# Pairing 64-row matmuls in the first product of a float32r feed-forward

## The chip, the cores and the metric

The kernel runs on one core of one Trainium2 chip. The metric is device time in microseconds (us) of one execution; a smaller number is better. TensorE does the matmuls, VectorE (DVE), ScalarE (ACT) and GpSimd (POOL) the elementwise work, and SyncE (SP) issues most of the DMAs.

## The reference

```python
def _moe2_ref(x, w_in, w_out):                    # the part that is changed
    h = np.maximum(x @ w_in, 0.0)                 # x: 3072 x 320, w_in: 320 x 2048
    return (h * h @ w_out).astype(np.float32)     # w_out: 2048 x 320

def reference(**kwargs):
    attn_out = _attn_ref(**attn_kwargs)           # a recurrence over 768 steps, 4 x 8 heads of 40
    x = attn_out, as 3072 tokens x 320
    x = _moe_ref(x=x, **moe_kwargs)               # first feed-forward: (x@w1 * x@w2) @ w3 @ w_out
    return _moe2_ref(x=x, **moe2_kwargs)          # second feed-forward
```

All inputs are float32.

## The kernel before, in words

The program has three parts that overlap at their seams: the recurrence in chunks of 32 steps, the first feed-forward, whose matmuls are laid between the chunks, and the second feed-forward at the end. The change is in the second one and in the preparation of its weights.

**Numbers in two parts.** Matmuls of the feed-forwards run in float32r. For accuracy each operand is split into a high and a low part, and a product is three matmuls: high by high, high by low, low by high.

**The first product.** The 320 rows of contraction are 128 + 128 + 64. Each of the two blocks of 128 rows takes three matmuls (tiles `wih`, `wil` for the weights, `xh`, `xl` for the data). The last 64 rows share one tile: `wir` holds on its 128 partitions the high part of 64 rows of weights and the low part of the same 64 rows. For the first 1024 hidden units the high part lies on partitions 0 to 63, for the other 1024 on partitions 64 to 127; the low part lies on the other half. `xq[:, 0]` holds the high part of the data's last 64 rows on both halves, and `xq[:, 1]` the low part on both halves. So `wir` by `xq[:, 0]` gives high by high plus low by high, and `wir` by `xq[:, 1]` gives high by low plus low by low. That makes eight matmuls (the helper `dense`, line 370) into one PSUM bank `ph` of 128 hidden units by 512 tokens.

**The loop.** It runs over `j` (6 groups of 512 tokens) and `ff` (16 blocks of 128 hidden units). `b_h(j, ff)` makes one `ph`; ScalarE takes the Relu out of it (`r_`, line 981), VectorE squares it (`q_`), ScalarE casts the square to the high part `rh`, VectorE subtracts for the low part `rl`. `b_o(j, ff)` adds the block's share to four accumulators `po` of 128 tokens by 320, three matmuls of 320 columns for each (line 997). `b_o` follows `b_h` by LAG = 3 blocks. There are four banks for `ph` and four for `po`. After the last block of a group of tokens the four `po` banks are copied out to `ob` (line 1007), two copies on VectorE and two on ScalarE, before the next group of tokens may write them.

**Who sets the order.** In the first parts TensorE's order is written by hand. In the second feed-forward the framework's planner sets it at build time: by a model of times it takes, for each engine, the earliest instruction in program order whose inputs and banks it holds to be ready. An engine then runs its instructions in that fixed order and waits where one is not ready.

**Weight preparation.** Before the loop, eight chunks of 256 hidden units are fetched and split (`split_w` for `wih` and `wil`, `wu` for the second product's `wuh` and `wul`). A chunk takes GpSimd, ScalarE and VectorE instructions on its way. `split_r` prepares 256 columns of each half of `wir` at a time, in the first four of the eight chunks. This work shares its engines with the end of the first feed-forward, whose matmuls are released between the chunks by `fill.pull`.

**Matmuls on a part of the array.** The recurrence has matmuls with a `tile_position`, which use only a part of the rows or columns of the array: line 772 (104 rows by 64 columns, two column tiles in turn), line 597 (40 rows by 32 columns, eight tiles: two halves of the rows, `tile_position=(64 * y, 32 * b)`, with y changing fastest, by four groups of columns). They are in float32, where one `matmul` call appears as two MATMUL rows in the trace.

Of the kernel before, what the change touches and what calls it, by code (L numbers as in the profile page):

```python
# [7 lines left out]
F32 = mybir.dt.float32  # L8
# [14 lines left out]
NU = B * H  # L23
HZ = H // 2
LAG = 3
LEAST, MOST = 0.25, 2.0

OPENING = (
# [35 lines left out]
LOOK = (1, 0, 2, 1, 5, 2)  # L64
# [179 lines left out]
def body(tc, img, rv, rd, vn, vp, raw, w1, w2, w3t, wo, win, wo2, ident, maskt, out, dbg=None):  # L244
    nc = tc.nc
    mm = nc.tensor.matmul
    act, dve, pool, sp = nc.scalar, nc.vector, nc.gpsimd, nc.sync

    with (
# [12 lines left out]
        with right, tc.manual_schedule(engines={mybir.EngineType.PE}):  # L262
# [99 lines left out]
            def dense(ps, w_, ff, xh, xl, xq, i0=0, i1=8):  # L362
                h, l, r = w_
                f = slice(128 * ff, 128 * ff + 128)
                seq = []
                for k in range(2):
                    seq += [(h[:, k, f], xh[:, k]), (h[:, k, f], xl[:, k]), (l[:, k, f], xh[:, k])]
                seq[5:5] = [(r[:, f], xq[:, 0]), (r[:, f], xq[:, 1])]
                for i in range(i0, i1):
                    mm(out=ps, lhsT=seq[i][0], rhs=seq[i][1], start=(i == 0), stop=(i == 7))  # L370
# [544 lines left out]
            wih = wb.tile([128, 2, FB], F32R, name="wih")  # L915
            wil = wb.tile([128, 2, FB], F32R, name="wil")
            wir = wb.tile([128, FB], F32R, name="wir")
            wuh = wb.tile([128, 16, DM], F32R, name="wuh")
            wul = wb.tile([128, 16, DM], F32R, name="wul")
            xt = {}  # L920
# [25 lines left out]
            wst = tc.alloc_tile_pool(name="wst", bufs=1, side="left")  # L946
            early = False
            bufs.update(raw=BB[0], wst=BB[1])
            for j in range(8):
                for k in range(2):  # L950
                    split_w(wst, win, wih, wil, j, k)
                if j < 4:
                    split_r(wst, [(win, 256 * j + 1024 * i, wir) for i in range(2)])
                for k in (2 * j, 2 * j + 1):
                    wu(wst, k)
                if j == 0:
                    b_split(wb, 0, 1)
                fill.pull(BP)
            fill.pull()
# [2 lines left out]
        with (  # L962
            left,
            tc.tile_pool(name="mb", bufs=1, side="right") as mb,
            tc.tile_pool(name="ps_h", bufs=4, space=PSUM) as ps_h,
            tc.tile_pool(name="ps_o", bufs=1, space=PSUM) as ps_o,
        ):
            NB = NTOK // 512
            tc.mark_branch_hint_location("wide", hint="LikelyTaken",
                                         engines=[mybir.EngineType.SP, mybir.EngineType.Activation,  # L970
                                                  mybir.EngineType.DVE])
            rr, last = {}, []

            def b_h(j, ff):
                ps = ps_h.tile([128, 512], F32, name="ph")
                dense(ps, (wih, wil, wir), ff, *xt[j])
                r_ = mb.tile([128, 512], F32, name="r_", bufs=2)
                q_ = mb.tile([128, 512], F32, name="q_", bufs=2)
                rh = mb.tile([128, 512], F32R, name="rh", bufs=4)
                rl = mb.tile([128, 512], F32R, name="rl", bufs=4)  # L980
                act.activation(out=r_, in_=ps, func=AF.Relu)
                dve.tensor_tensor(out=q_, in0=r_, in1=r_, op=ALU.mult)
                last[:] = [act.copy(out=rh, in_=q_).ins,
                           dve.tensor_tensor(out=rl, in0=q_, in1=rh, op=ALU.subtract).ins]  # L984
                rr[ff] = (rh, rl)

            po = {}

            def b_o(j, ff, gs=range(4)):
                if ff == 0:  # L990
                    po[j] = [ps_o.tile([128, DM], F32, name=f"po{g}") for g in range(4)]
                rh, rl = rr[ff]
                for g in gs:
                    t = slice(128 * g, 128 * g + 128)
                    for i, (a_, b_) in enumerate(((rh[:, t], wuh[:, ff]), (rh[:, t], wul[:, ff]),
                                                  (rl[:, t], wuh[:, ff]))):
                        mm(out=po[j][g], lhsT=a_, rhs=b_, start=(ff == 0 and i == 0), stop=(ff == 15 and i == 2))  # L997
                if ff == 15:
                    for g in gs:
                        c = 4 * j + g  # L1000
                        if j < NB - 1:
                            ob = mb.tile([128, DM], F32, name="ob", bufs=4)
                        else:
                            if g == 0:
                                po["ob"] = mb.tile([128, 4, DM], F32, name="oball", bufs=1)
                            ob = po["ob"][:, g]
                        (act.copy if g % 2 else dve.tensor_copy)(out=ob, in_=po[j][g])
                        if j < NB - 1:
                            sp.dma_start(out=out.rearrange("(b s) o -> b s o", b=B)[:, C * c:C * c + C], in_=ob)
                    if j == NB - 1 and gs[-1] == 3:  # L1010
                        for b in range(B):
                            (act if b % 2 else sp).dma_start(
                                out=out.rearrange("(b c s) o -> b s c o", b=B, s=C)[b][:, 4 * j:4 * j + 4],
                                in_=po["ob"][C * b:C * b + C])

            NW = 8
            nw = NU * S * D // 128 // NW
            low, high = (mb.tile([128, NW], F32, name=n, bufs=1) for n in ("low", "high"))

            def look(i):  # L1020

                w_ = mb.tile([128, nw], F32, name="w_", bufs=2)
                sp.dma_start(out=w_, in_=raw[3].rearrange("u s d -> (u s d)").rearrange("(p f) -> p f", p=128)[
                    :, nw * i:nw * i + nw])
                for o, op in ((low, ALU.min), (high, ALU.max)):
                    with tc.issue_after(last[1]):
                        dve.tensor_reduce(out=o[:, i:i + 1], in_=w_, axis=mybir.AxisListType.X, op=op)
                    yield

            def within():  # L1030


                with tc.issue_after(last[1]):
                    for o, op in ((low, ALU.min), (high, ALU.max)):
                        dve.tensor_reduce(out=o[:, 0:1], in_=o, axis=mybir.AxisListType.X, op=op)
                    dve.tensor_scalar(out=high[:, 0:1], in0=high[:, 0:1], scalar1=MOST, scalar2=None, op0=ALU.is_le)
                    dve.scalar_tensor_tensor(out=low[:, 0:1], in0=low[:, 0:1], scalar=LEAST, in1=high[:, 0:1],
                                             op0=ALU.is_ge, op1=ALU.mult)
                row = mb.tile([1, 128], F32, name="row", bufs=1)
                sp.dma_start(out=ok_d, in_=low[:, 0:1])  # L1040
                sp.dma_start(out=row, in_=ok_d.rearrange("p o -> o p"))
                for _ in range(4):
                    yield
                one = mb.tile([1, 1], mybir.dt.int32, name="one", bufs=1)
                with tc.issue_after(last[1]):
                    dve.tensor_reduce(out=row[:, 0:1], in_=row, axis=mybir.AxisListType.X, op=ALU.min)
                    dve.tensor_copy(out=one, in_=row[:, 0:1])
                yield one

            def guard():  # L1050

                for i in range(NW):
                    yield from look(i)
                yield from within()

            lag, steps, fast = [], guard(), None
            for j in range(NB):
                for ff in range(16):
                    if (j, ff) == LOOK[4:6]:
                        fast = nc.values_load(fast, min_val=0, max_val=1)  # L1060
                    if ff == 4 and j + 1 < NB:
                        b_load(mb, j + 1)
                    if ff == 12 and j + 1 < NB:
                        with tc.issue_after(last[0]), tc.issue_after(last[1]):
                            b_split(mb, j + 1)
                    b_h(j, ff)
                    if LOOK[0:2] <= (j, ff) and ff % LOOK[2] == LOOK[3]:
                        fast = next(steps, fast)
                    lag.append((j, ff))
                    if len(lag) > LAG:  # L1070
                        b_o(*lag.pop(0))
            for g in range(4):
                with tc.high_priority(offset=FIRST * (4 - g)):
                    for it in lag:
                        b_o(*it, gs=(g,))
# [61 lines left out]
```

## Time and profile before

| what | value |
|---|---|
| median of 3 runs | 1070.16 us (1068.26 to 1074.72) |
| the profiled execution's own time | 1071.28 us |
| its span, first to last instruction | 1069.5 us |
| TensorE busy | 918.1 us, 86% of the span |
| VectorE, ScalarE, GpSimd busy | 712.5, 443.8, 233.2 us |
| mean granted TensorE clock | 0.961 |

Times in the rows are microseconds from the start of the span, unless marked ns. PE is TensorE's matmul stream, PEld its weight loads. Matmuls are pipelined and their ends are modelled, so a row's own duration is longer than the pitch at which matmuls follow one another; the pitch is read from the starts.

### The profile page before, as it was taken

How to read it: one execution, taken by the hardware profiler on the slowest of the kernel's cores; microseconds unless marked ns; L12 is line 12 of the kernel's file. 1: busy time of each engine (PE TensorE's matmuls, PEld its weight loads, DVE VectorE, ACT ScalarE, POOL GpSimd, SP SyncE). 2: the span in 40 equal slices, each digit the busy share in tenths (PEclk: the TensorE clock that was granted, in tenths of full speed). 3: DMA queues.
4: the chain of work that ended last, by engine and by line, in shares of the span. 5: the costliest groups of instructions: out<-in, count | busy, mean ns of one | idle time of the engine just before them, and what ended most of it. 6: DMA issues, size and time to landing. Idle time of an engine off the chain costs nothing.

```text
span 1069.5 us, 29225 instructions
## 1 busy us (share of the span) xinstructions
PE 918.1 (86%) x12240; PEld 822.5 (77%) x12240; DVE 712.5 (67%) x1399; ACT 443.8 (41%) x942; POOL 233.2 (22%) x304
## 2 busy tenths in 40 slices
PE   1327777688989889979899999889999999999997
PEld 1315545588888878979798889868989898898896
DVE  6864879957975997798489444887456554444432
ACT  2424556343434423424343434775334333333332
POOL 0271224433343343533200000652000000000000
PEclk9999888899999999989899999989999999999999
DMA  8976785666666567766644542665122121000001
GB/s 212 307 235 177 209 247 158 171 168 170 163 154 173 148 151 182 170 170 149 164 118 110 136 96 60 171 188 111 30 62 53 59 48 25 2 25 1 18 8 28
DMA packets 208922, 134.45 MB, mean 126 GB/s; under 512 B 143741, under 2 KB 184062, under 8 KB 208368
## 3 DMA queue, kind: packets, MB, share of 16 engines
q1 hardware_dynamic: 201424, 110.61, 40.6%
q0 software_dynamic: 7072, 21.57, 7.1%
q8 instruction: 99, 1.62, 0.7%
q10 hardware_dynamic: 288, 0.33, 0.2%
q14 instruction: 39, 0.32, 0.1%
HBM read 99.27 MB, written 33.19 MB: 124 GB/s over the span
## 4 chain that ended last, share of the span: by engine, by line
PE 48%; DVE 26%; DMA 12%; issue 5%; ACT 4%; POOL 3%; SPq 2%; ACTq 0%; DVEq 0%; POOLq 0%
PE ph L370 16%; PE po L997 15%; PE ab L370 6%; DMA im<-img 5%; DVE tmp L656 4%; PE px L428 4%; DVE T L659 4%; PE pat L800 2%; DVE RX L808 2%; DVE yst L812 2%; DVE gl L408 2%; DVE g L402 1%; DVE wst L328 1%; DVE YI L777 1%; POOL im L584 1%
## 5 line engine op out<-in xcount | busy, mean ns | idle before, releaser
L997 PE MATMUL po<-wul,rh 128*128 128x320 f32 x384 | 118.3, 308 | 0.0
L997 PE MATMUL po<-wuh,rh 128*128 128x320 f32 x384 | 118.0, 308 | 0.0
L997 PE MATMUL po<-wuh,rl 128*128 128x320 f32 x384 | 116.9, 308 | 0.0
L407 ACT CAST gh<-g 128x256 fp32r<-128x256 f32 x96 | 39.0, 406 | 99.8 <-DVE g L402 86.5
L370 PE MATMUL ph<-xh,wih 128*128 128x512 f32 x192 | 76.0, 396 | 0.7 <-issue 0.7
L428 PE MATMUL px<-wph,gh 128*128 128x320 f32 x192 | 68.1, 355 | 9.3 <-DVE x L433 4.8
L370 PE MATMUL ph<-xh,wil 128*128 128x512 f32 x192 | 75.7, 394 | 0.0
L370 PE MATMUL ph<-xl,wih 128*128 128x512 f32 x192 | 75.6, 394 | 0.0
L997 PEld LDWEIGHTS po<-wul,rh 128*128 128x128 f32 x384 | 72.0, 188 | 4.2
L997 PEld LDWEIGHTS po<-wuh,rh 128*128 128x128 f32 x384 | 72.0, 188 | 3.8
L997 PEld LDWEIGHTS po<-wuh,rl 128*128 128x128 f32 x384 | 71.6, 188 | 0.6 <-DVE rl L984 0.6
L800 PE MATMUL pat<-YI,YR 128*40 128x72 f32 (+1 forms) x1536 | 58.8, 240 | 13.7 <-DVE qt L602 8.1
L800 PEld LDWEIGHTS pat<-YI,YR 128*40 128x40 f32 x1536 | 54.5, 127 | 19.2 <-DVE qt L602 9.7
L408 DVE TENSOR_TENSOR gl<-g,gh 128x256 fp32r<-128x256 f32 x96 | 48.2, 503 | 30.0 <-ACT gh L407 29.6
L401 ACT COPY a_sb<-ab 128x256 f32<-128x256 f32 x96 | 35.6, 371 | 76.4 <-PE ab L370 75.9
L656 DVE TENSOR_TENSOR tmp<-PT,T 128x31 f32<-128x31 f32 (+20 forms) x170 | 64.9, 382 | 3.4
L659 DVE TENSOR_TENSOR T<-T,tmp 128x31 f32<-128x31 f32 (+20 forms) x170 | 64.5, 380 | 3.0
L428 PE MATMUL px<-wph,gl 128*128 128x320 f32 x192 | 63.2, 329 | 3.4 <-DVE gl L408 3.4
L584 POOL TENSOR_TENSOR im<-im,suf 104x256 f32<-104x256 f32 x80 | 64.4, 836 | 0.0
L428 PE MATMUL px<-wpl,gh 128*128 128x320 f32 x192 | 62.4, 325 | 0.0
L370 PE MATMUL ph<-xq,wir 128*128 128x512 f32 x192 | 60.1, 394 | 0.0
L370 PE MATMUL ab<-xh,w1h 128*128 128x256 f32 x192 | 57.9, 302 | 2.5 <-ACT xh L357 2.2
(539 smaller groups left out, 2444.3 us busy)
## 6 DMA issues: line engine op xcount, KB each, us to landing
raw<-w3t SPq DMA_DIRECT2D x16, 512.0 KB
YR<-KB_d SPq DMA_DIRECT2D x48, 160.0 KB
im<-img POOLq DMA_DIRECT2D x28, 240.0 KB, 4.5
wt<-AW_d SPq DMA_DIRECT2D x24, 214.5 KB
raw<-wo SPq DMA_DIRECT2D x16, 320.0 KB
RX<-vp SPq DMA_DIRECT2D x24, 208.0 KB
vs<-rv SPq DMA_DIRECT2D x24, 208.0 KB
KB_d<-kn POOLq DMA_DIRECT2D x14, 320.0 KB, 5.3
```

Of the source, the lines that this page charges most:

```text
L370: mm(out=ps, lhsT=seq[i][0], rhs=seq[i][1], start=(i == 0), stop=(i == 7))
L401: act.copy(out=a_sb, in_=ps[:, 0])
L407: act.copy(out=t["gh"][:, ff], in_=g)
L408: dve.tensor_tensor(out=t["gl"][:, ff], in0=g, in1=t["gh"][:, ff], op=ALU.subtract)
L428: mm(out=ps, lhsT=a_, rhs=b_, start=(k == 0 and i == 0), stop=(k == 7 and i == 2))
L584: eng.tensor_tensor(out=kb[:, g, :, :, j], in0=kb[:, g, :, :, j], in1=sg, op=ALU.mult)
L656: dve.tensor_tensor(out=tv, in0=Pv[:, :, s, s + 1:n].unsqueeze(3).to_broadcast(sh), in1=Tv[:, :, s, 0:s + 1].unsqueeze(2).to_broadcast(sh) ...
L659: return dve.tensor_tensor(out=o, in0=o, in1=tv, op=ALU.subtract).ins
L800: mm(out=ps[64 * y:64 * y + D, b, 72 * z:72 * z + n], lhsT=YR[:, u], rhs=YI[:, u, 0:n], start=True, stop=True, tile_position=(0, 64 * y))
L808: dve.tensor_tensor(out=o, in0=v[r, :, :, C:72], in1=decay.unsqueeze(3).to_broadcast([D, 2, HZ, D]), op=ALU.mult)
L812: dve.tensor_tensor(out=yst[r, :, 2 * g:2 * g + 2].rearrange("p z b t -> p b z t"), in0=v[r, :, :, 0:C], in1=wt[c][r, 2 * g:2 * g + 2, :, ...
L997: mm(out=po[j][g], lhsT=a_, rhs=b_, start=(ff == 0 and i == 0), stop=(ff == 15 and i == 2))
```

## The change: pairs of 64-row matmuls, four blocks at a time

The eighth matmul, `wir` by `xq[:, 1]` over 128 rows, is replaced by a matmul over the 64 rows that hold the high part of the weights alone (the low by low share is left out of the sum). `tile_position` places it on the upper or the lower half of the array's rows. Blocks are visited in a new order (`ORDER`: 0, 8, 1, 9, 2, 10, ...), so that neighbours have their high parts on different halves. At every fourth block `b_r` takes all four `ph` banks and issues the four 64-row matmuls of the next four blocks, upper, lower, upper, lower, as the ones that start the accumulation. The other seven matmuls of each block follow in `b_h` as before. The chunks of weights are prepared in the order 0, 4, 1, 5, 2, 6, 3, 7, with `split_r` at every second one.

```diff
+ORDER = tuple(f + 8 * h for i in range(0, 8, 2) for f in (i, i + 1) for h in range(2))
...
-            for j in range(8):
+            for m in range(8):
+                j = m // 2 + 4 * (m % 2)
                 for k in range(2):
                     split_w(wst, win, wih, wil, j, k)
-                if j < 4:
+                if m % 2 == 0:
                     split_r(wst, [(win, 256 * j + 1024 * i, wir) for i in range(2)])
                 for k in (2 * j, 2 * j + 1):
                     wu(wst, k)
...
-            def b_h(j, ff):
-                ps = ps_h.tile([128, 512], F32, name="ph")
-                dense(ps, (wih, wil, wir), ff, *xt[j])
+            def b_r(j, n):
+                for m in range(n, n + 4):
+                    ph[m] = ps_h.tile([128, 512], F32, name="ph")
+                for m in range(n, n + 4):
+                    r = slice(64 * (m % 2), 64 * (m % 2) + 64)
+                    mm(out=ph[m], lhsT=wir[r, 128 * ORDER[m]:128 * ORDER[m] + 128], rhs=xt[j][2][r, 1],
+                       start=True, stop=False, tile_position=(64 * (m % 2), 0))
+
+            def b_h(j, n):
+                if n % 4 == 0:
+                    b_r(j, n)
+                ps, ff = ph.pop(n), ORDER[n]
+                f = slice(128 * ff, 128 * ff + 128)
+                xh, xl, xq = xt[j]
+                seq = [(wir[:, f], xq[:, 0])]
+                for k in range(2):
+                    seq += [(wih[:, k, f], xh[:, k]), (wih[:, k, f], xl[:, k]), (wil[:, k, f], xh[:, k])]
+                for i, (a_, b_) in enumerate(seq):
+                    mm(out=ps, lhsT=a_, rhs=b_, start=False, stop=(i == 6))
...
-                rr[ff] = (rh, rl)
+                rr[n] = (rh, rl)
...
-                for ff in range(16):
+                for n in range(16):
...
-                    b_h(j, ff)
+                    b_h(j, n)
```

`b_o` takes its weights at `ORDER[n]` and starts and stops the accumulation at n = 0 and n = 15.

## Rows read from the trace of the kernel before

**Rows 1.** The page: the span, and each engine's busy time

```profile
span 1069.5 us, 29225 instructions
PE 918.1 (86%) x12240; PEld 822.5 (77%) x12240; DVE 712.5 (67%) x1399; ACT 443.8 (41%) x942; POOL 233.2 (22%) x304
```

**Rows 2.** Busy time by stretch: length, each engine, granted clock, DMA share, GB/s

```profile
700.00:716.00 16.00, 11.13 (x45) 9.22 (x45) 13.24 (x26) 11.37 (x32) 9.24 (x10) 0.79 0.56 175
716.00:732.00 16.00, 15.95 (x82) 13.70 (x81) 15.65 (x24) 13.21 (x32) 6.91 (x8) 1.00 0.98 214
732.00:1062.00 330.00, 330.00 (x1830) 297.34 (x1830) 159.09 (x230) 123.06 (x205) 2.04 (x2) 1.00 0.13 30
```

**Rows 3.** The chain that ended last, 912 to 916: start, duration, what

```profile
912.05 1.87 PE ph L370 x8
913.92 1.76 PE po L997 x12
```

**Rows 4.** Groups by shape: line 772, busy, mean ns

```profile
L772 PE MATMUL pat<-RT,vs 104*64 104x64 f32 x768 | 29.3, 233 | 6.1 <-ACT vs L761 5.9
```

**Rows 5.** TensorE's timeline around one run of line 772: start, duration

```profile
387.25 0.28 PE L370 MATMUL ab<-xh,w1l 128*128 128x256 f32 x1
387.37 0.28 PE L370 MATMUL ab<-xh,w1h 128*128 128x256 f32 x1
387.57 1.15 PE L772 MATMUL pat<-RT,vs 104*64 104x64 f32 x32
388.65 0.39 PE L370 MATMUL ab<-xl,w1h 128*128 128x256 f32 x1
388.88 0.41 PE L370 MATMUL ab<-xq,w1r 128*128 128x256 f32 x2
```

**Rows 6.** TensorE's timeline around one run of line 597

```profile
393.50 0.85 PE L597 MATMUL pat<-im 40*32 40x64 f32 x64 [0.58 <-DVE YI L777]
394.27 0.39 PE L370 MATMUL ab<-xl,w2h 128*128 128x256 f32 x1
394.50 0.41 PE L370 MATMUL ab<-xq,w2r 128*128 128x256 f32 x2
```

**Rows 7.** Timeline of a regular block, ScalarE and TensorE

```profile
913.52 0.40 PE L370 MATMUL ph<-xh,wil 128*128 128x512 f32 x1
914.02 0.60 ACT L981 ACTIVATE r__12360<-ph 128x512 f32<-128x512 f32 x1 [1.65 <-PE ph L370]
915.52 0.40 PE L370 MATMUL ph<-xh,wih 128*128 128x512 f32 x1
```

**Rows 8.** Timeline where the accumulators change from tokens 0 to 1

```profile
777.64 0.40 PE L370 MATMUL ph<-xh,wih 128*128 128x512 f32 x1
...
778.17 0.42 ACT L1007 COPY ob<-po 128x320 f32<-128x320 f32 x1
...
779.28 0.39 PE L370 MATMUL ph<-xh,wil 128*128 128x512 f32 x1
779.51 0.39 PE L370 MATMUL ph<-xh,wih 128*128 128x512 f32 x1
...
781.15 0.31 PE L997 MATMUL po<-wuh,rh 128*128 128x320 f32 x1
```

**Rows 9.** Timeline of the loop's start, TensorE

```profile
714.08 0.47 PE L370 MATMUL ph<-xh,wih 128*128 128x512 f32 x1 [0.66 <-issue]
...
714.61 0.39 PE L370 MATMUL ph<-xh,wil 128*128 128x512 f32 x1
714.84 0.39 PE L370 MATMUL ph<-xh,wih 128*128 128x512 f32 x1
...
724.81 0.31 PE L997 MATMUL po<-wuh,rh 128*128 128x320 f32 x1
```

**Rows 10.** Timeline of the loop's start, ScalarE

```profile
720.25 0.61 ACT L983 CAST rh<-q__10605 128x512 fp32r<-128x512 f32 x1
...
724.14 0.61 ACT L981 ACTIVATE r__10655<-ph 128x512 f32<-128x512 f32 x1
```

More of the change, by code (lines that the diff above doesn't have):

```diff
@@ L955, in body @@
                     wu(wst, k)
-                if j == 0:
+                if m == 0:
                     b_split(wb, 0, 1)
@@ L984, in b_h, with b_o @@
                            dve.tensor_tensor(out=rl, in0=q_, in1=rh, op=ALU.subtract).ins]
-                rr[ff] = (rh, rl)
-            po = {}
-            def b_o(j, ff, gs=range(4)):
-                if ff == 0:
+                rr[n] = (rh, rl)
+            po, ph = {}, {}
+            def b_o(j, n, gs=range(4)):
+                ff = ORDER[n]
+                if n == 0:
                     po[j] = [ps_o.tile([128, DM], F32, name=f"po{g}") for g in range(4)]
-                rh, rl = rr[ff]
+                rh, rl = rr[n]
                 for g in gs:
@@ L996, in b_o @@
                                                   (rl[:, t], wuh[:, ff]))):
-                        mm(out=po[j][g], lhsT=a_, rhs=b_, start=(ff == 0 and i == 0), stop=(ff == 15 and i == 2))
-                if ff == 15:
+                        mm(out=po[j][g], lhsT=a_, rhs=b_, start=(n == 0 and i == 0), stop=(n == 15 and i == 2))
+                if n == 15:
                     for g in gs:
@@ L1057, in body @@
             for j in range(NB):
-                for ff in range(16):
-                    if (j, ff) == LOOK[4:6]:
+                for n in range(16):
+                    if (j, n) == LOOK[4:6]:
                         fast = nc.values_load(fast, min_val=0, max_val=1)
-                    if ff == 4 and j + 1 < NB:
+                    if n == 4 and j + 1 < NB:
                         b_load(mb, j + 1)
-                    if ff == 12 and j + 1 < NB:
+                    if n == 12 and j + 1 < NB:
                         with tc.issue_after(last[0]), tc.issue_after(last[1]):
                             b_split(mb, j + 1)
-                    b_h(j, ff)
-                    if LOOK[0:2] <= (j, ff) and ff % LOOK[2] == LOOK[3]:
+                    b_h(j, n)
+                    if LOOK[0:2] <= (j, n) and n % LOOK[2] == LOOK[3]:
                         fast = next(steps, fast)
-                    lag.append((j, ff))
+                    lag.append((j, n))
                     if len(lag) > LAG:
```

## The prediction

> **What bounds the kernel now.** I read the page first: TensorE is busy for 86% of the span, more than any other engine [rows 1]. An average over stages decides nothing, so the table by stretch came next. From 732 to 1062 us TensorE is busy for all of 330 us at a granted clock of 1.00, while VectorE and ScalarE work for 159 and 123 us [rows 2]. The chain of waits agrees: there it runs from TensorE to TensorE, eight matmuls into `ph` in 1.87 us, then twelve into `po` in 1.76 us, with nothing between [rows 3]. So in the loop of the second feed-forward each nanosecond of TensorE's is one of the kernel's, and there alone the change works. The loop's first 16 us are nearly as full, 15.95 of 16 [rows 2], but there ScalarE and VectorE are full too (13.21 and 15.65), with weight preparation. Before it, from 700 to 716, TensorE idles for 4.9 us.
>
> **The change, part by part.**
>
> *The unit price.* A full 512-column matmul costs 1.87 / 8 = 0.234 us of TensorE. There are 6 x 16 = 96 blocks, so 24 groups of four. A group gives up four full matmuls, 4 x 0.234 = 0.934 us, and gets four 64-row ones.
>
> *Do two halves run at the same time?* No row of before shows float32r on a half. Line 597 uses two halves of the rows by four groups of columns, in float32. First what one such matmul costs its tile: line 772's 32 rows take 1.15 us [rows 5], the last of them 0.23 [rows 4], so the pitch is (1.15 - 0.23) / 31 = 0.030; two column tiles take turns, so a 64-column one holds its tile for 0.059. Line 597 has the same 64 columns, and passes 64 of them in the 0.77 us from its first start to the next line's [rows 6]: 64 x 0.059 / 0.77 = 4.9 at once. Four groups of columns alone give four, so the halves overlapped. I take that over for float32r: two pairs cost 2 x 0.234 = 0.467. The bounds are 4 x 0.234 = 0.934 (one after the other) and 2 x 0.227 = 0.454 (the pitch at the loop's start: 45 matmuls from 714.61 to the first `po` at 724.81 [rows 9]).
>
> *What going into the part-array mode and out of it costs.* Around line 772, from the last full matmul's start (387.37) to the second full one's after it (388.88) is 1.51 us [rows 5]. Two full matmuls at 0.12 (387.25 to 387.37) and 16 turns of 0.059 explain 0.24 + 0.95 = 1.19, so 0.32 us is lost at the two seams. A part of it can be seen: the first full matmul after the block is followed after 0.23 instead of 0.12, and after line 597 it is 0.23 again [rows 6], so about 0.11 us is the load of 128 columns of weights that no longer hides behind the matmul ahead. Line 772 loads 64 columns on its way in, the change loads 128 on both ways, so I take between 0.32 and 0.43, and settle on 0.40.
>
> The Trainium skill has a rule that speaks against this change: "TensorEngine Tiling (Array Packing)", Tiling Modes, Key Properties, says that a change of tiling mode, not merely of tile, drains the engine. The trace agrees with it by the 0.32 us above. Another page of the Trainium skill, "TensorE: Matmul & The Clock Gate", Part 3, gives a pack of tiles as one matmul's duration plus some 4 ns for each further tile, with no charge for the seams. By that formula alone a group would cost an estimated 0.47 us; the trace does not bear it out.
>
> *A regular group* then costs 0.40 + 0.467 = 0.867 against 0.934: 0.067 us gained. Half of the four matmuls' time is saved, 0.467, and 0.40 is paid back for one trip into the half-array mode.
>
> *The four banks.* `b_r` claims all four `ph` banks together, so its fourth matmul waits for the Relu of the block just finished; before, a block waited for a Relu three blocks old. In a regular place the cover is enough: a block's last matmul starts at 913.52, its Relu runs from 914.02 to 914.62, and the next block's first matmul comes at 915.52, after twelve matmuls into `po` [rows 7]. That leaves 0.9 us. Behind the waiting matmul stands all of TensorE's queue, so if the cover goes, it costs that wait directly.
>
> *The cover is gone where the accumulators change.* There the planner held `b_o` of the new tokens' block 0 for not ready (its banks are still being copied out, the fourth copy at 778.17), and put matmuls of two blocks in a row: from 777.64 over 779.28, where block 3's last one starts, and on with block 4 from 779.51, with `po` only at 781.15 [rows 8]. After the change the next work in program order behind block 3 is `b_r` of blocks 4 to 7. Three of its matmuls have free banks. The fourth waits for block 3's Relu, which starts some 0.1 us after that block's end and takes 0.60 [rows 7], while the three take about 0.47. So the planner fills in full matmuls of block 4, and the fourth goes alone: two trips, 0.867 + (0.40 + 0.234) = 1.50 us against 0.934. That is 0.57 lost, at the five changes of tokens: 2.8 us. The bounds: 0.067 gained each, if the planner waits and the Relu is early; 0.57 lost.
>
> *The loop's start.* Block 0's group finds free banks. For the second group TensorE arrives at 714.08 + 0.87 + 28 x 0.227 = 721.3, and block 3's Relu ended at 724.75 in the trace, because ScalarE was full [rows 10]. Before, TensorE filled this time with blocks 4 and 5 and first came to `po` at 724.81 [rows 9]. Now it has the high parts of block 0's `po` (its `rh` is ready at 720.86 [rows 10], 8 x 0.147 = 1.2 us) and blocks 4 and 5, if `b_r` is taken apart. I charge one extra trip as above, 0.57; bounds 0.07 gained, and 3.4 lost (nothing fills it).
>
> *The order of the weight chunks.* Block n needs chunk number n / 2 as before, only under other names, so supply does not get later; two of four `split_r` move from ahead of the loop to its first 16 us. What that shifts in the end of the first feed-forward is the planner's affair. Its bound is the idle time there, 4.9 us of 16 [rows 2], gained or lost in part; I take 0 and keep 2 us to either side. The DMA count is unchanged.
>
> *The sum*, against the profiled execution's own 1071.28 us: 18 regular groups, 18 x 0.067 = -1.2; five token changes, +2.8; the start, +0.6; chunks 0. Together +2.2, 1073.5. The median of the runs is 1.1 us under the profiled one, so on its scale 1072.4; I say **1073**.
>
> **The rivals.**
>
> *The seams stay whole.* The planner keeps each `b_r` together everywhere. Then 24 x 0.067 = 1.6 us are gained, 1069.7; with 0.32 for a trip and 0.227 for a pair, 24 x (0.934 - 0.774) = 3.8, 1067.4. For it: all regular blocks follow program order. Against: the token changes in the trace are out of it [rows 8].
>
> *The halves do not overlap in float32r*, and the change doesn't do what it says. Then a group costs 0.40 + 0.934 and the kernel becomes **slower**: 24 x 0.40 = 9.6, 1080.9, and with six more trips of 0.40, 1083.3. It decides from a pair's time: above (0.934 - 0.40) / 2 = 0.267 us, in place of 0.234, even a regular group loses. For it: no row with float32r on half an array. Against: line 597 [rows 6].
>
> *The seams cost nothing*: the weights of the first pair, and of the first full matmul after it, load behind the matmul ahead, and the two pairs' 0.467 us are the whole price of a group. 24 x 0.467 = 11.2 us gained, 1060.1. Against it stand the 0.32 us around line 772 and the 0.11 at each return [rows 5, 6]. The formula of the Trainium skill's "TensorE: Matmul & The Clock Gate", Part 3, would give this case.
>
> **How the numbers follow.** Chances: the forecast 0.63 (1071 to 1076), whole seams 0.19, no overlap 0.13, free seams 0.04, something else 0.01. The range of 8 in 10 has to take in the whole-seams case with the chunks' 2 us below it, down to 1067, and above the start's 3.4 us and the lower part of no overlap, up to 1081. About 1%, 10.7 us, is what a measurement of this kernel can tell from no change. Only free seams come out faster by more than that, 0.04; the upper half of no overlap and a little else slower, 0.09; the rest, 0.87, within it.
>
> **What would show it.** In the profile after: rows of 64 by 128 into `ph`, 96 of them, whose starts come in pairs a few ns apart (right) or 0.23 apart (no overlap); from the last `po` start before a regular group to the second full matmul after it about 0.15 + 0.867 + 0.234 us; lone 64-row matmuls right behind the five token changes; and a period of four blocks of about 14.45 us in place of 14.52. If every group is whole, the forecast is 3 to 4 us too high; if the first `ph` row moves by more than 2 us, the chunks' order was mis-sized.

## The result, and the profile after

| | before | after |
|---|---|---|
| median of 4 runs each, same chip | 1072.44 us (1068.26 to 1075.07) | 1089.12 us (1083.71 to 1090.82) |
| profiled execution, its span | 1071.28, 1069.5 us | 1090.35, 1088.6 us |
| first `ph` matmul starts | 714.1 us | 718.0 us |
| last `po` matmul starts | 1062.2 us | 1081.1 us |
| from the one to the other ("the loop" below) | 348.1 us | 363.1 us |
| from there to the span's end | 7.3 us | 7.5 us |

The ratio is 1.0146, with a 95% interval of 1.0108 to 1.0184: slower, by 16.7 us between the medians, where 1073 was forecast and 1081 was the upper end of the range. In the profiled executions the spans differ by 19.1 us. Of that 15.0 lie inside the loop, 3.9 ahead of it, 0.2 behind it.

The page of the kernel after answers to [rows 1]. Over the same 12240 matmul rows TensorE is busy for 13.5 us longer; the other engines stay within 2 us:

```profile
span 1088.6 us, 29225 instructions
PE 931.6 (86%) x12240; PEld 814.1 (75%) x12240; DVE 712.0 (65%) x1399; ACT 443.4 (41%) x942; POOL 235.1 (22%) x304
```

The table by stretch, with the columns of [rows 2], gives the place. First the start of the loop, then 300 us of it:

```profile
700.00:716.00 16.00, 12.34 (x64) 10.82 (x63) 15.36 (x30) 12.73 (x35) 8.87 (x10) 0.79 0.55 160
716.00:732.00 16.00, 14.57 (x66) 10.74 (x65) 14.53 (x22) 13.11 (x35) 9.90 (x11) 1.00 0.85 201
760.00:1060.00 300.00, 300.00 (x1588) 252.64 (x1587) 139.67 (x200) 106.86 (x178) 0.00 (x0) 1.00 0.12 30
```

TensorE is still shown busy for all of the 300 us, at a granted clock of 1.00, but it gets through 1588 matmuls: 5.29 per us, where before had 1660 in its own 300 us from 760 to 1060, 5.53 per us. The line of before for that stretch:

```profile
760.00:1060.00 300.00, 300.00 (x1660) 269.87 (x1660) 142.80 (x205) 109.92 (x183) 0.00 (x0) 1.00 0.12 28
```

So TensorE does not wait for another engine; its own stream takes longer, although half of 96 full matmuls' time was meant to be gone. "Busy" doesn't tell this apart, the count beside it does.

The chain of waits answers to [rows 3] (start, duration, what). A regular place:

```profile
817.07 1.76 PE po L1016 x12
818.83 0.66 PE ph L981 x3
819.49 1.83 PE ph L994 x7
821.32 0.30 PE po L1016 x2
821.62 0.42 PE ph L981
822.04 1.66 PE po L1016 x10
823.70 1.64 PE ph L994 x7
```

Line 981 is the 64-row matmul of `b_r`, line 994 the block's seven others, line 1016 `b_o`. The group of four is not together: three go, then a whole block and two `po` matmuls, then the fourth alone. TensorE's timeline of the same place shows what each trip costs:

```profile
818.38 0.31 PE L1016 MATMUL po<-wul,rh 128*128 128x320 f32 x1
818.52 0.30 PE L1016 MATMUL po<-wuh,rl 128*128 128x320 f32 x1
818.76 0.73 PE L981 MATMUL ph<-xq,wir 64*128 64x512 f32 x3
819.42 0.50 PE L994 MATMUL ph<-xq,wir 128*128 128x512 f32 x1
819.76 0.39 PE L994 MATMUL ph<-xh,wih 128*128 128x512 f32 x1
...
821.31 0.31 PE L1016 MATMUL po<-wul,rh 128*128 128x320 f32 x1
821.55 0.49 PE L981 MATMUL ph<-xq,wir 64*128 64x512 f32 x1
821.97 0.41 PE L1016 MATMUL po<-wuh,rl 128*128 128x320 f32 x1
822.22 0.30 PE L1016 MATMUL po<-wuh,rh 128*128 128x320 f32 x1
```

Read the starts. The lone matmul comes 0.24 us after the `po` ahead of it (0.147 is the pitch), the next `po` 0.42 after that (0.234 would be its own time), and the one behind 0.25 (again 0.147): 0.09 + 0.19 + 0.10 = 0.38 us for the way in and out, and 0.234 for the matmul. The trip of three loses the same: 0.09, then 0.66 instead of the 0.467 of two pairs, then 0.34 instead of 0.234. I price a trip as the time from the last full matmul's start ahead of it to the second full one's behind it, less the two pitches. Of the 54 trips of this trace, 17 of three cost 0.856 us (median), 5 of two 0.611, 31 of one 0.618; the loop's first group stands behind an idle stretch and has no such price.

Was the fourth bank late? ScalarE's timeline has the Relu that frees it:

```profile
817.17 0.60 ACT L999 ACTIVATE r__11417<-ph 128x512 f32<-128x512 f32 x1 [1.41 <-PE ph L994]
```

It ends at 817.77, 1.0 us before the three start and 3.8 before the fourth does. No wait in the trace put the fourth where it is. The order did, which the planner had fixed at build time.

Where the accumulators change, the group falls into three trips, of two, one and one; here the first two, and the third behind the turn to `po`:

```profile
847.08 0.49 PE L981 MATMUL ph<-xq,wir 64*128 64x512 f32 x2
847.50 0.50 PE L994 MATMUL ph<-xq,wir 128*128 128x512 f32 x1
...
848.39 0.49 PE L981 MATMUL ph<-xq,wir 64*128 64x512 f32 x1
848.81 0.50 PE L994 MATMUL ph<-xh,wil 128*128 128x512 f32 x1
...
851.70 0.49 PE L981 MATMUL ph<-xq,wir 64*128 64x512 f32 x1
852.12 0.41 PE L1016 MATMUL po<-wuh,rh 128*128 128x320 f32 x1
```

At the loop's start the first group is whole and the second goes as four singles. Together 1 + 4 + 17 x 2 + 5 x 3 = 54 trips, where the forecast had 30.

### The profile page after: what moved, and what is told of

Read it like the earlier page. It is cut to its first block, busy times and chain, and to the rows that moved or that the text cites. A ratio compares the mean times of both kernels' runs of the same rounds, so it can differ in the third digit from the quotient of the medians.

```text
span 1088.6 us, 29225 instructions
## 1 busy us (share of the span) xinstructions
PE 931.6 (86%) x12240; PEld 814.1 (75%) x12240; DVE 712.0 (65%) x1399; ACT 443.4 (41%) x942; POOL 235.1 (22%) x304
## 4 chain that ended last, share of the span: by engine, by line
PE 47%; DVE 23%; DMA 16%; ACT 5%; issue 4%; POOL 2%; SPq 2%; ACTq 0%; DVEq 0%; POOLq 0%
PE po L1016 16%; PE ph L994 14%; PE ab L371 6%; DVE tmp L657 4%; DVE T L660 4%; DMA im<-img 3%; PE px L429 3%; PE pat L801 2%; PE ph L981 2%; DMA raw<-w3t 2%; DVE RX L809 2%; DVE yst L813 2%; DMA AW_d<-wi 2%; DMA raw<-win 2%; DMA X_d<-yst 1%
## 5 line engine op out<-in xcount | busy, mean ns | idle before, releaser
L801 PE MATMUL pat<-YI,YR 128*40 128x72 f32 (+1 forms) x1536 | 61.9, 247 | 16.2 <-DVE qt L603 9.1
L801 PEld LDWEIGHTS pat<-YI,YR 128*40 128x40 f32 x1536 | 57.4, 132 | 21.7 <-DVE qt L603 10.8
L657 DVE TENSOR_TENSOR tmp<-PT,T 128x31 f32<-128x31 f32 (+20 forms) x170 | 67.6, 398 | 3.4
L409 DVE TENSOR_TENSOR gl<-g,gh 128x256 fp32r<-128x256 f32 x96 | 44.5, 463 | 29.2 <-ACT gh L408 28.8
L371 PE MATMUL ab<-xl,w1h 128*128 128x256 f32 x192 | 57.9, 301 | 2.1 <-DVE xl L359 2.0
```

Of the source, the lines that this page charges most:

```text
L409: dve.tensor_tensor(out=t["gl"][:, ff], in0=g, in1=t["gh"][:, ff], op=ALU.subtract)
L657: dve.tensor_tensor(out=tv, in0=Pv[:, :, s, s + 1:n].unsqueeze(3).to_broadcast(sh), in1=Tv[:, :, s, 0:s + 1].unsqueeze(2).to_broadcast(sh) ...
L801: mm(out=ps[64 * y:64 * y + D, b, 72 * z:72 * z + n], lhsT=YR[:, u], rhs=YI[:, u, 0:n], start=True, stop=True, tile_position=(0, 64 * y))
```

## The experiments

My theory after the result: the loss is trips into the half-array mode. Each has the forecast's price, the planner's order makes 54 of 24, and the chip needs none of the 30 extra. The rivals: the new order in itself costs (four banks claimed ahead, three and one apart), mode or not; the new order of the weight chunks delays the loop (it starts 3.9 us later); the chip needs the spread order, so that keeping a group together only brings a wait for the fourth bank. "The loop" is again the time from the first `ph` start to the last `po` start of the profiled execution.

| run | ratio to before, 95% | loop, us | trips |
|---|---|---|---|
| after | 1.0146 (1.0108 to 1.0184) | 363.1 | 54 |
| e1, chunk order only | 0.9995 (0.996 to 1.003) | 347.9 | 0 |
| e2, grouped, full rows | 0.9989 (0.9964 to 1.0014) | 348.5 | 0 |
| e3, after by hand order | 0.9979 (0.9952 to 1.0006) | 347.0 | 27 |
| e4, group later, planned | 1.0042 (1.0013 to 1.0072) | 352.2 | 37 |
| e5, four on one half | one run, 1078.86 us | 357.8 | 27 |
| e6, two at a time | one run, 1079.84 us | 356.8 | 50 |
| e7, before by hand order | 1.0008 (0.9978 to 1.0038) | 348.7 | 0 |
| e8, hand order from the second tokens | 0.9972 (0.9946 to 0.9999) | 346.2 | 20 |

Beside e1 to e4, run together, before had a median of 1075.95 us; beside e5 to e8, 1073.61. The ratios are not the quotients of these medians (for e1 that quotient is 0.9973, inside its interval). The four kernels that change no mode in the loop (before, e1, e2, e7) have loops of 347.9 to 348.7 us, so a difference of half a microsecond in this column tells nothing. A finer measure is the time from the last `po` start of the first 512 tokens to the last of the fifth, which leaves out both ends of the loop: 232.24 us in before (777.50 to 1009.74), 232.24 in e1, 231.80 in e2, 232.32 in e7, 230.56 in e3 and in e8, 242.19 in after.

**e1: the order of blocks and chunks alone.** The eight full matmuls are back.

```diff
-                if n % 4 == 0:
-                    b_r(j, n)
-                ps, ff = ph.pop(n), ORDER[n]
...
+                ps, ff = ps_h.tile([128, 512], F32, name="ph"), ORDER[n]
+                dense(ps, (wih, wil, wir), ff, *xt[j])
```

> Only the order of the weight chunks and of the blocks is changed; every block keeps its eight full matmuls, nothing is grouped and nothing runs on half the array. Theory A (the loss is trips into the half-array mode, made more numerous by the planned order): the loop, from the first ph matmul to the last po matmul, lasts 348 us as before, against 363 after the change. What the chunk order itself costs shows in the start of the first ph matmul: 714.1 before, 718.0 after; here 714 to 718, so the time is 1071 to 1076. Rival C (the new order of the chunks or of the blocks is what costs): 1085 or more, with the loop above 355.

1073.07 us, ratio 0.9995; the first `ph` starts at 715.5 and the loop takes 347.9. The order of the chunks is not what costs. The start itself varies: 718.0, 715.5, 716.6, 717.1, 718.9 and 712.7 in after, e1 to e4 and e6, which have the new chunk order; 714.1, 711.9, 717.9 and 716.7 in before, e5, e7 and e8, which have the old one. The two lists overlap over most of their length, so the 3.9 us between the two first profiles are not shown to be the change's.

**e2: the groups, without the half-array mode.** `b_r` stays, with full rows.

```diff
-                    mm(out=ph[m], lhsT=wir[r, 128 * ORDER[m]:128 * ORDER[m] + 128], rhs=xt[j][2][r, 1],
-                       start=True, stop=False, tile_position=(64 * (m % 2), 0))
+                    mm(out=ph[m], lhsT=wir[:, 128 * ORDER[m]:128 * ORDER[m] + 128], rhs=xt[j][2][:, 1],
+                       start=True, stop=False)
```

> The changed kernel with its grouping by four, its banks and its order, but the four matmuls of a group are over all 128 rows, without a place on half the array (so the low-by-low share is in the sum again). Theory A (trips): no mode changes, so the loop falls back from 363 to 348 or 349 us and the time is 1071 to 1076. Rival B (claiming four banks at once makes TensorE wait, whatever the matmuls are): the loop stays at 360 or more, 1086 or above.

1073.93 us, ratio 0.9989, loop 348.5. The planner spreads the group in the same way: compared one by one, by the names of their tiles, the 1920 matmuls into `ph` and `po` come in the same order as in after. TensorE's timeline of e2:

```profile
799.05 0.30 PE L1016 MATMUL po<-wuh,rl 128*128 128x320 f32 x1
799.19 0.86 PE L981 MATMUL ph<-xq,wir 128*128 128x512 f32 x3
799.89 0.40 PE L994 MATMUL ph<-xq,wir 128*128 128x512 f32 x1
...
801.67 0.31 PE L1016 MATMUL po<-wul,rh 128*128 128x320 f32 x1
801.82 0.40 PE L981 MATMUL ph<-xq,wir 128*128 128x512 f32 x1
802.05 0.31 PE L1016 MATMUL po<-wuh,rl 128*128 128x320 f32 x1
```

The three start 0.14 after the `po` and take 0.70 = 3 x 0.234; the lone one stands 0.15 behind its `po` and 0.23 ahead of the next. With full rows the seams are gone and the spread order costs nothing. So claiming four banks and splitting the group are harmless by themselves; a split costs because each part changes the mode.

**e3: after, with TensorE's order as the program has it.** From the loop's ninth block on the planner no longer sets TensorE's order.

```diff
+            hand = ExitStack()
             for j in range(NB):
                 for n in range(16):
+                    if (j, n) == (0, 8):
+                        hand.enter_context(tc.manual_schedule(engines={mybir.EngineType.PE}))
...
+            hand.close()
```

> The changed kernel with TensorE's order taken from the program from block 8 of the first tokens on, so that the four matmuls of a group stand together: 27 trips in place of 54. Theory A: a whole trip costs about 0.86 us against 0.934, the 22 groups gain some 0.07 each, the start keeps its five trips (+1.5 us), and the Relu is in time: loop 347.5 to 349 us, time 1071 to 1077. Rival B (the fourth bank really comes late, and the planner was right to spread the four): TensorE waits at each group, 22 times 1 us or more, loop above 365, time above 1088.

1073.73 us, ratio 0.9979, loop 347.0, 16.1 us less than after and 0.5 under the range expected. There are 27 trips, 23 of four at 0.854 us and, at the loop's start, 4 of one at 0.614. ScalarE's and TensorE's timelines of e3 show that the fourth bank is there in time:

```profile
812.35 0.60 ACT L999 ACTIVATE r__11419<-ph 128x512 f32<-128x512 f32 x1 [1.40 <-PE ph L994]
```

```profile
813.70 0.30 PE L1016 MATMUL po<-wuh,rl 128*128 128x320 f32 x1
813.93 0.73 PE L981 MATMUL ph<-xq,wir 64*128 64x512 f32 x4
814.60 0.50 PE L994 MATMUL ph<-xq,wir 128*128 128x512 f32 x1
814.93 0.40 PE L994 MATMUL ph<-xh,wih 128*128 128x512 f32 x1
...
828.34 0.73 PE L981 MATMUL ph<-xq,wir 64*128 64x512 f32 x4
```

The Relu ends at 812.95, the four follow at 813.93, 0.23 us behind the `po` as in every trip, and take 0.67 until the next full matmul: no wait beyond the seam. The period of four blocks is 828.34 - 813.93 = 14.41 us, against 14.52 before and 833.87 - 818.83 = 15.04 after. The rival by which the chip needs the spread order falls.

**e7: the hand order without the change.** Before, with the same lines from (0, 8) on.

```diff
+                    if (j, ff) == (0, 8):
+                        hand.enter_context(tc.manual_schedule(engines={mybir.EngineType.PE}))
```

> The kernel before with TensorE's order taken from the program from block 8 of the first tokens on; nothing else. Theory A: the order alone is worth nothing when there are no mode changes; the loop stays at 348.1 us within 0.3, the time within 0.5% of before. Rival E (the hand order is what gained in e3, by removing the planned order's shifts at the token changes): the loop falls to 347 or below.

1074.00 us, ratio 1.0008. The loop of 348.7 is 0.3 us beyond what was expected, but the excess lies at its ends: over the four groups of tokens between them it is 232.32 us against 232.24 before. By itself the hand order is worth nothing, so e3's return comes from the whole groups.

**e4: the planner left in charge, more work ahead of the group.** Two blocks' `b_o` are pulled ahead of each group.

```diff
+                    while n % 4 == 0 and len(lag) > 1:
+                        b_o(*lag.pop(0))
                     b_h(j, n)
```

> The changed kernel with two more of the second product's blocks set ahead of each group of four in program order (the backlog is worked off down to one block before b_r), the order still planned. In the planned order 17 groups are whole, the five token changes make three trips each, and the start five: 37 trips. Theory A: 17 x -0.07, five x (3 x 0.62 - 0.93) = +4.6, start +1.5: loop 352.5 to 353.5 us, time 1075 to 1081. Rival B (a wait for the bank, not trips): with 5 us of cover nothing waits, so the loop would be 348 or below.

1080.28 us, ratio 1.0042, loop 352.2, 0.3 under the range expected. All 17 regular groups stay whole, and the first, as here on TensorE's timeline:

```profile
747.11 0.30 PE L1016 MATMUL po<-wuh,rl 128*128 128x320 f32 x1
747.35 0.73 PE L981 MATMUL ph<-xq,wir 64*128 64x512 f32 x4
748.00 0.50 PE L994 MATMUL ph<-xq,wir 128*128 128x512 f32 x1
```

The five token changes still make three trips each and the start five: 17 + 15 + 5 = 37, which is the number in the trace (18 of four at 0.856, 14 of one at 0.618, 5 of two at 0.610). With 24 more `po` matmuls ahead, 24 x 0.147 = 3.5 us, the planner holds the fourth bank for free. So it judges by the bank, it seems, but with a time of its own, later than the chip's: by more than the 1.0 us that the Relu of after ends ahead of the three, or the group would stay whole there, and by less than some 5 us (1.0, the 3.5, and the half microsecond in which the four start). The order in after narrows this. By the rule that the planner takes the earliest instruction it holds to be ready, the bank came free for it between the matmul just ahead of the fourth and the fourth itself. In the regular places these start 3.5 and 3.8 us after the end of the Relu that frees the bank (821.31 and 821.55 against 817.77); at the token changes the third and the fourth matmul of the group also start 3.8 to 3.9 us after theirs. An estimate of the lateness from these starts is thus 3.5 to 3.8 us; the planner's own times are in no trace.

**e6: two blocks at a time.** `b_r` is called at every second block, for two.

```diff
-                for m in range(n, n + 4):
+                for m in range(n, n + 2):
...
-                if n % 4 == 0:
+                if n % 2 == 0:
```

> The changed kernel with two blocks at a time instead of four: the banks asked for were left two and three blocks ago. Planned order. Theory A (the planner split the fours because of the fourth bank alone): pairs stay together, in 46 trips of two, and each costs about 0.62 us against 0.467; with four lone ones at the start (+1.5) the loop lasts 348.1 + 46 x 0.15 + 1.5 = 356.5 us. If a trip cost nothing beyond its matmuls: 348.1 - 46 x 0.234 = 337.

One run, 1079.84 us; loop 356.8. Outside the start all 46 pairs stay whole, because a pair's second bank hangs on a Relu two blocks older than the one just finished. So what the planner splits on is how young the bank's Relu is. A pair's trip costs 0.622 us, and two pairs 1.24 against 0.934: with so little on it, a trip can't pay.

**e5: four on the same half.** The old order of blocks and chunks, and the hand order of e3 (both left out of the cut below); a group's four matmuls all lie on one half of the array.

```diff
-                    r = slice(64 * (m % 2), 64 * (m % 2) + 64)
+                    r = slice(64 * (m // 8), 64 * (m // 8) + 64)
...
-                       start=True, stop=False, tile_position=(64 * (m % 2), 0))
+                       start=True, stop=False, tile_position=(64 * (m // 8), 0))
```

> The order by hand of e3, but blocks in their natural order, so that the four 64-row matmuls of a group all lie on the same half of the array (weight chunks in their old order too). Theory A (the two halves work at the same time, and that halves the four): a trip is now about 0.39 + 4 x 0.234 = 1.32 us in place of 0.85, 23 groups of four pay 0.467 more each, the loop goes from 347.0 to about 357.8 us. Rival D (halves do not overlap; e3 gained for another reason, such as fewer rows): the loop stays within 1 us of 347.

One run, 1078.86 us; loop 357.8. TensorE's timeline of e5:

```profile
766.59 0.30 PE L1015 MATMUL po<-wuh,rl 128*128 128x320 f32 x1
766.82 1.20 PE L980 MATMUL ph<-xq,wir 64*128 64x512 f32 x4
767.95 0.50 PE L993 MATMUL ph<-xq,wir 128*128 128x512 f32 x1
768.29 0.39 PE L993 MATMUL ph<-xh,wih 128*128 128x512 f32 x1
```

From the first of the four to the next full one it is 1.13 us, where e3 has 0.67: 0.46 more, two matmuls of 0.234; 23 x 0.467 = 10.7 us is also what the loop takes longer than e3's (357.8 - 347.0). The trip costs 1.320 us. So on two halves the four take two matmuls' time, on one half four: the overlap is real, and the 0.38 of the seams is the same in both (1.320 - 4 x 0.234, 0.854 - 2 x 0.234).

**e8: only whole groups.** The first 512 tokens are done as before, with the old chunk order; from the second on come `b_r` and the hand order (the chunk order is left out of the cut below).

```diff
+                if j == 0:
+                    ps = ps_h.tile([128, 512], F32, name="ph")
+                    dense(ps, (wih, wil, wir), n, *xt[j])
+                else:
+                    if n % 4 == 0:
+                        b_r(j, n)
...
+                    if (j, n) == (1, 0):
+                        hand.enter_context(tc.manual_schedule(engines={mybir.EngineType.PE}))
```

> A version made from the findings: the first 512 tokens as before (eight full matmuls, natural order, weight chunks in their old order), from the second 512 tokens on groups of four on both halves with TensorE's order by hand: 20 whole trips. Theory A: each saves what e3's period shows, 14.52 - 14.40 = 0.12 us, so the loop lasts 348.1 - 2.3 = 345.8 us, and the time is 0.2% under before. Rival B (waits for the fourth bank at the token changes): loop above 348.

1070.69 us, ratio 0.9972 (0.9946 to 0.9999), loop 346.2. Its 20 trips are whole and cost 0.854 each, at the changes of the accumulators too. TensorE's timeline of e8 where they change to the third 512 tokens, the place at which after made three trips:

```profile
841.24 0.30 PE L1019 MATMUL po<-wuh,rl 128*128 128x320 f32 x1
841.47 0.73 PE L980 MATMUL ph<-xq,wir 64*128 64x512 f32 x4
842.14 0.50 PE L997 MATMUL ph<-xq,wir 128*128 128x512 f32 x1
```

The kernel is 0.3% under before, with an interval that ends just short of 1 and overlaps those of e2 and e3, so by its time alone the gain is hardly shown. In the loop 20 x (0.934 - 0.854) = 1.6 us were to be won, and 348.1 - 346.2 = 1.9 are seen. Over the four groups of tokens between the ends, 230.56 us stand against 232.24 to 232.32 in before, e1 and e7: 1.7 us on 16 trips, of which 16 x 0.080 = 1.3 are the trips' and 0.4 is there with full rows too (e2).

## Why the prediction was wrong

**The step that failed** is "In a regular place the cover is enough", and with it the row of 18 regular groups at -0.067. I took the cover from the trace: the Relu ends 0.9 us early, so the group runs through. On the chip that is so (1.0 us in after, and no wait in e3). But the group is laid out by the planner, and its model held the fourth bank for late. I had named this rule myself, that the planner takes what it *holds* to be ready, and applied it to the token changes alone, where the trace of before showed its effect; for the regular places I put the trace's times in the planner's place. Before, no block claimed a bank younger than three blocks, so that trace shows no `ph` bank held for late. It does show it of the `po` banks: in [rows 8] the fourth copy ends at 778.59 (778.17 + 0.42), and the first `po` is placed at 781.15, 2.56 us later. So it is at all five token changes, and in e7, in program order, the `po` comes 0.91 us behind that copy with no wait. The prediction took this place for copies that are late on the chip. Read as the planner's lateness, which is argued and not tried, it would not have let 0.9 us of cover stand.

The terms, as forecast and as measured, with a full matmul at 0.234 and so a group at 0.934 before:

| term | forecast | measured |
|---|---|---|
| trip of four or three | 0.867 | 0.855 |
| trip of one | 0.634 | 0.618 |
| regular groups | 18 x -0.067 = -1.2 | 17 x (0.856 + 0.618 - 0.934) - 0.08 = +9.1 |
| token changes | 5 x 0.57 = +2.8 | 5 x (0.611 + 2 x 0.618 - 0.934) = +4.6 |
| start | +0.6 | 4 x 0.618 - 0.934 = +1.5 |
| chunk order | 0 ± 2 | no effect seen (e1) |
| sum in the loop | +2.2 | +15.2 worked out, +15.0 read off |

The -0.08 is the first group, which stayed whole (0.854 - 0.934). The sum leaves 0.2 us, so nothing else in the loop is needed to explain the loss.

**What held.** The unit price of a trip: 0.40 for the seams was forecast, from line 772's 0.32 and the 0.11 of a return, and 0.38 came. The reason for going above 0.32 held as well: on the way in, line 772's second pair, with 64 columns of weights, starts 0.11 us after its first in place of 0.06, and in e3 the second pair, with 128, 0.34 in place of 0.23, so 0.05 us are lost there and 0.10 here. The overlap of the halves in float32r, taken over from line 597 in float32, is shown by e5 against e3. The rule of the Trainium skill's "TensorEngine Tiling (Array Packing)", Tiling Modes, Key Properties, that a change of mode drains the engine and a change of tile does not, is borne out by the cost: 0.38 us for each trip, whatever stands on it; that it is a drain no row shows by itself. The formula of "TensorE: Matmul & The Clock Gate", Part 3, of the Trainium skill leaves the seams out, and its estimate of 0.47 us for a group stands against 0.854 measured; the rival of free seams falls.

**The token changes** went apart at the bank, as forecast, but into three trips and not two: the planner held the third bank for late as well, since two blocks had just gone without `po` between them. The forecast had the chip's Relu as the reason; the third matmul starts 3.9 us after the Relu that it needs had ended, so here too the reason is the planner's time. **The start**: blocks 4 to 7 went as four singles, not as three and one. Both are the same mistake as the regular places, smaller.

**The rival of whole seams** is what the chip would have allowed. With the hand order it came out as forecast for it: 0.080 us per group measured, between the 0.067 and 0.160 worked out there.

**The sign by which to notice it.** "If every group is whole, the forecast is 3 to 4 us too high" was written down; that every regular group might be split was not among the rivals, and with something else at 0.01 it had next to no chance, though the same arithmetic gives it: 18 further trips of 0.634 are 11.4 us. The first `ph` row moved by 3.9 us, beyond the 2 at which I would have called the chunk order mis-sized; e1 and the scatter of the starts say that this sign was a poor one.

**What stays open.** Why the planner's model holds the banks for late was not tried: e6 ties it to the youngest banks, e4 bounds it to between 1 and 5 us, and the order in after puts it at some 3.5 to 3.8. Nor is it known what moves the loop's start between 711.9 and 718.9 us from one execution to the next.

## What to carry to other kernels

A part-array matmul pays by what rides on each change of mode: at the 0.38 us a trip of this kernel, with 512 columns and a granted clock of 1.00, four 64-row matmuls win 0.08 us, two lose 0.15, a single one loses 0.38. So the group has to stay together, and where a planner orders an engine, whether it does is decided by the planner's times for the banks, not by the trace's: look at the order it would lay, and write it by hand where a split costs. And when a stretch shows an engine 100% busy before and after, compare the instructions per us.

## What the runs showed of the hardware that was not expected

The price of a trip doesn't depend on where the odd matmul stands: three cost 0.856 and four 0.854 us, one 0.618 and two 0.611 to 0.622, since a half that is left empty saves nothing. And each of the two changes of mode loses time in two places. TensorE's timeline of e3, asked for in windows so narrow that the four matmuls are not merged, with the weight loads (PEld) beside it:

```profile
813.56 0.19 PEld L1016 LDWEIGHTS po<-wuh,rl 128*128 128x128 f32 x1
813.70 0.30 PE L1016 MATMUL po<-wuh,rl 128*128 128x320 f32 x1
813.93 0.30 PEld L981 LDWEIGHTS ph<-xq,wir 64*128 64x128 f32 x4 [0.19 <-issue]
813.93 0.50 PE L981 MATMUL ph<-xq,wir 64*128 64x512 f32 x2
814.27 0.40 PE L981 MATMUL ph<-xq,wir 64*128 64x512 f32 x2
814.60 0.19 PEld L994 LDWEIGHTS ph<-xq,wir 128*128 128x128 f32 x1 [0.37 <-issue]
```

The two of a pair start together, as forecast for halves that overlap. The first pair is 0.09 us late and the second 0.10 (0.34 after the first in place of 0.234); the full matmul at 814.60 is 0.09 late and the next, at 814.93, 0.10. In a trip of one the second and the third of these fall together: the 0.19 us behind the lone matmul. The weights show a part of it: those of the last `po` load from 0.14 us ahead of it, those of the first pair and of the first full matmul only from the matmul's own start.
